# A pre-norm block with Hedgehog linear attention: where six query sums are inverted, and a new order for the first half

## The chip, the cores and the metric

The kernel runs on one core of a Trainium2 chip. The core has five engines with a queue of instructions each: TensorE (PE) multiplies matrices, VectorE (DVE), ScalarE (ACT) and GpSimd (POOL) do the rest of the arithmetic, and SyncE (SP) starts the transfers (DMAs). Each queue runs strictly in its own order; an instruction waits until the semaphores of what it needs have arrived, and everything behind it in the same queue waits with it. The metric is the device time of one execution in microseconds (us), lower being better.

## The reference

The input is 2048 tokens of width 640 in bfloat16. The block is an attention half and a feed-forward half, each with a residual:

```python
def _A_ref(x, wqkv, w_phi, wo):                  # 32 heads of 20
    q, k, v = split(x @ wqkv)
    pq = jnp.einsum("bhsd,hdf->bhsf", q, w_phi)
    pk = jnp.einsum("bhsd,hdf->bhsf", k, w_phi)
    phi_q = concat([softmax(pq), softmax(-pq)])  # 40 features a head
    phi_k = concat([softmax(pk), softmax(-pk)])
    kv = jnp.einsum("bhsf,bhsd->bhfd", phi_k, v)
    z  = jnp.einsum("bhsf->bhf", phi_k)
    num = jnp.einsum("bhqf,bhfd->bhqd", phi_q, kv)
    den = jnp.einsum("bhqf,bhf->bhq", phi_q, z)[..., None] + 1e-6
    return (num / den) @ wo
def _B_ref(x, w1, w2): return silu(x @ w1) @ w2  # 640 -> 1728 -> 640
h  = x + _A_ref(layernorm(x), ...)
h2 = h + _B_ref(layernorm(h), ...)
```

Because the output is a ratio, a common factor of the two halves of phi_q cancels. The kernel therefore leaves the positive exponentials of a query as they are and multiplies the negative ones by (sum of the positive ones) / (sum of the negative ones). That ratio is what the change is about: one number for each of 32 heads (33 columns with a padding head) and token.

## The kernel before, in words

The tokens are cut into 16 tiles of 128. The work of a tile is cut into named steps, and the whole program is one list of step names, `ORDER`. The list is walked once, each name issues its instructions to the queues, and the order in the list is the order within every queue. Nothing reorders it later. A table `ON` says for some steps on which engine they run. A number behind a name is the tile.

- Loading and norm. `X0, X1, X2, X4, X8` load the tokens (L161; `X8` brings tiles 8 to 15 in one transfer), `WKc` and `WVc` the weights (L164), `load0` to `load11` the rest (L488), all from SP's queue. `st` takes mean and variance on VectorE (L432, L433). `rs` is the inverse deviation: on GpSimd an addition and a power (L441, L444), on ScalarE a logarithm and an exponential (L438, L439). `xn` normalizes (L448), on VectorE or on GpSimd. `xt` transposes the tile: for tiles 0 to 3 on TensorE (L455) with a copy `x` behind it (L475), for the others by a DMA from SP's queue (L477).
- Folding weights. w_phi is multiplied into the key and the query weights before use. For keys: `wk` transposes on TensorE (L290), `wke` evicts (L307), `fk` multiplies (L314), `fke` evicts (L323). For queries: `wq0` to `wq5` transpose columns of wqkv by DMA (L386), `phq` builds the block diagonal of w_phi, `fq0` to `fq5` multiply (L398), `fqe` evict (L404).
- Keys and values. `K` and `V` project a tile (L496; for tile 0 in five pieces `K0.c` L523 and `V0.c` L508). `ex` takes both exponentials on ScalarE (L551), `su` their sums on VectorE (L555), `rk` inverts the sums on ScalarE by logarithm and exponential (L563, L564), `sc` scales on VectorE (L568), `ve` evicts the values (L572). `kv` adds the tile into the sum over all tokens (L587), which stays in two PSUM banks. After tile 15, `bd0` and `bd1` mask it into block diagonals (L596, L598).
- Queries. `Q` projects (L534), `qe` takes the exponentials (L656), `qs` the sums (L660), and `qr` is three VectorE instructions: a reciprocal (L668), a product that gives the ratio in bfloat16 (L670), and the scaling of the negative exponentials (L678). `qt` transposes the features by DMA (L684). `D` multiplies them into the masked sum (L709), `E` divides on VectorE (L721, L722), `ot` transposes (L733), `G` projects (L742) and `ga` adds the residual into `X` (L749).
- Feed forward. `ls`, `lr` and `hn` normalize again (L432, L441, L448), `ht` transposes by DMA (L769). Tiles go in units 0 to 1, 2 to 5, 6 to 9, 10 to 13, 14 to 15. `u0.*`, `u2.*` and so on are up projections (L824, L835), `s` the silu on ScalarE (L844, L851), `lt` a transpose (L856), `d` the down projections (L864, L867), `oa` the last addition (L873), `out` the store (L878).

PSUM has eight banks. Up to the step `halves`, two hold the key-value sum, and every `wk` pair, `xt`, `fk`, `fq`, `K`, `V` and `Q` takes the next of three pairs in turn, so it waits until what was put there three allocations earlier has been evicted. From `halves` on, eight single banks go round. Tiles in SBUF have small rings of buffers too: four for exponentials of keys, two for the sums of queries.

The up projections of unit 0 (the first `u0` in the list) need `ht0` and `ht1`. From `u2.2` on, after `G61 d11 ht5`, the two lists below are the same.

Of the kernel before, what the change touches and what calls it, by code (L numbers as in the profile page):

```python
# [18 lines left out]
warm0 warm1 warm2 warm3 warm4 warm5 warm6 warm7 warm8 warm9 warm10 warm11 warm12 warm13 warm14 X0 WK2  # L19
ones0 wk2 warm15 warm16 warm17 warm18 warm19 WK3 wke2 WK0 X1 WK1 st0 wk3 phi_a wke3 wk0 phi_b rs0 xn0  # L20
wke0 own st1 xt0 wk1 fk3 WK4 wke1 X2 wk4 rs1 WV0 wke4 x0 fk1 X4 fk3e WV3 xn1 st2 st3 rs2 WV2 WV4 rs3 fk0
fk1e fk0e fk4 WV1 V0.0 xn3 xn2 wph1 fk4e fk2 fk2e st6 xt1 wq2 K0s K0.0 K0.4 K0.3 K0.2 K0.1 ones1 x1 st4
rs4 xt2 K1 ex0 V0.2 ones5 xn4 wq4 V0.3 V0.1 st5 x2 wph0 su0 ex1 su1 rs5 V0.4 K2 xn5 phq xt3 V1 rs6 ex2
V2 x3 st7 xn6 rk0 X8 su2 rs7 ve1 ve2 ve0 xt4 sc0 st8 V3 fq2 xt5 rk2 ve3 K3 xn7 st11 ones3 fq2e V4 K4 rk1
ex3 wq3 ones2 ve4 kv0 ones6 sc1 ones7 sc2 V5 fq3 rs8 st9 ex4 su3 st10 rs9 wq0 kv1 ve5 ones4 xt6 su4 K5
fq0 fq3e K6 rk3 ex5 xt7 kv2 wq1 wq5 fq1 fq0e sc3 ex6 K7 load6 su5 fq1e mask kv3 ex7 xn8 st13 V6 xt8
mask0 rk4 ve6 rk5 su6 sc4 rs11 fq4 fq4e xn9 zeros st12 V7 ve7 rk6 V8 rs10 sc5 xt9 xn10 load3 V9 su7 ve8
fq5 rs12 rs13 st14 ve9 xt10 kv4 fq5e rk7 load7 K8 ex8 sc6 kv5 st15 xn11 K9 su8 xn12 sc7 Q0 kv6 K10 xt11
kv7 ex9 Q1 rk8 rs15 load2 su9 xn13 qe0 ex10 qe1 K11 xt13 sc8 rs14 mask1 rk9 qs0 kv8 xt12 xn14 load11 V10
V13 qr0 ex11 su10 sc9 xn15 V11 su11 kv9 xt14 rk10 ve13 ve10 K12 load4 ve11 qs1 K13 qr1 xt15 eqp K14 ex12  # L30
rk11 sc10 su12 kv10 ex13 ex14 rk12 V12 load5 V14 sc11 su13 ve12 K15 su14 pad0 sc12 rk13 kv11 qt0 Q2 sc13
ve14 qt1 load0 rk14 ex15 qe2 kv12 sc14 load1 su15 V15 kv13 rk15 ve15 Q3 qs2 kv14 load9 sc15 kv15 qr2 Q5
Q7 bd1 bd0 qe3 qe5 halves D0 qs3 Q4 qt2 E00 E01 qe7 qe4 qr3 D1 Q6 E10 Q9 E11 Q8 qe6 qe9 qs4 qr4 qs5 Q10
ot0 qr5 qt3 Q11 ot1 qe8 qe10 D2 qe11 E20 G00 G01 ga00 E21 D3 E30 qt4 E31 ga01 G10 ga10 ot2 G11 ga11 Q14
Q12 qe14 ot3 ls0 D4 lr0 G20 Q13 ls1 G30 qe12 lr1 hn0 qt5 E40 G21 G31 hn1 E41 ht0 ht1 ga30 ga20 qs6 Q15
qe13 pad1 ga21 D5 ga31 qs7 qr6 u0.0 E50 u0.6 qe15 E51 ls3 qr7 ls2 s0.0 load8 u0.L s0.L s0.6 u0.10 ot4
u0.12 u0.8 lr3 G40 G41 lr2 s0.12 s0.10 u0.4 load10 hn3 qt6 ga41 ot5 ga40 u0.2 s0.8 ls4 D6 lt0 G50 qt7
E60 lr4 G51 E61 ht3 ga51 s0.2 s0.4 d10 D7 ga50 hn4 ls5 ot6 lr5 hn2 qs8 d00 E70 hn5 oa00 ht2 d01 G60 ht4
G61 qr8 oa10 d11 ht5 ga61 u2.2 u2.0 ga60 qt8 E71 ot7 s2.0 oa01 qs9 u2.L qs13 s2.2 qr9 oa11 qs11 u2.6 D8
u2.10 E80 ls6 qt9 u2.7 u2.3 s2.L u2.11 s2.10 s2.6 qr13 E81 u2.9 s2.9 qr11 u2.5 qs12 s2.7 qs10 s2.3 u2.1  # L40
D9 G70 s2.5 E90 qr10 u2.12 s2.11 E91 ot8 G71 u2.4 lr6 ga71 ga70 qt11 out0 lt2 s2.1 qt10 u2.8 out1 hn6
s2.4 qr12 ls7 G80 s2.8 ga80 ot9 G81 D11 s2.12 E110 d30 ht6 qt13 E111 d20 D10 ga81 lr7 G90 E100 oa30 oa20
E101 ot10 G91 hn7 ga91 d31 ot11 ga90 ls8 qs15 lr8 d21 qt12 oa31 d50 G100 ls9 G101 hn8 out3 d40 d51 ht8
# [10 lines left out]
s14.8 out12 d140 d141 oa140 d150 oa141 out14 d151 oa150 out150 d152 oa151 out151 oa152 out152
# [4 lines left out]
def kernel(  # L59
# [603 lines left out]

    def query_ratio(t):
        n = HC * NCH
        s3 = sq.pop(t)[:].rearrange("p c (h b) -> p (c h) b", b=2)
# [1 line left out]
        nc.vector.reciprocal(rm[:], s3[:, :, 1])  # L668
# [1 line left out]
        nc.vector.tensor_tensor(  # L670
            r2[:],
            s3[:, :, 0].unsqueeze(2).to_broadcast([P, n, 2]),
            rm[:].unsqueeze(2).to_broadcast([P, n, 2]),
            op=ALU.mult,
        )
# [265 lines left out]
```

## Time and profile before

| | us |
|---|---|
| median of 3 runs | 237.36 |
| lowest and highest run | 237.30, 237.70 |
| the profiled execution | 236.82 |
| its span (first to last record) | 234.8 |
| busy in the span: PE, DVE, ACT, POOL | 229.5, 165.8, 105.1, 64.4 |

The profile is of one execution. A row of a timeline begins with the start and the duration in us; a row of the chain too. A row of a group ends with the count, then the busy time in all, the mean of one in ns, and the idle time in front. Durations of neighbours on one engine overlap slightly, so their sums come out a little too long. Matmuls are pipelined and their ends are modelled; what counts for PE is when it starts something and what it had to wait for.

### The profile page before, as it was taken

What the parts mean: (1) busy time and instruction counts of PE and PEld (TensorE: products, weight loads), DVE (VectorE), ACT (ScalarE), POOL (GpSimd) and SP (SyncE); (2) the same over time, 40 slices, a digit from 0 to 9 for tenths busy, and PEclk for the clock granted to TensorE, in tenths of its full rate; (3) what the DMA queues carried; (4) which work ended last, traced back from release to release, by engine and by line L of the source; (5) the groups of instructions that cost most, each with busy time, mean ns of one, the idle gap of its engine ahead of it and who ended that gap; (6) DMA issues with size and microseconds to landing.
All of it is one profiled execution on the core that took longest, in us unless ns stands there. A gap on an engine that the chain in (4) does not pass through costs nothing.

```text
span 234.8 us, 5031 instructions
## 1 busy us (share of the span) xinstructions
PE 229.5 (98%) x1984; PEld 161.2 (69%) x1984; DVE 165.8 (71%) x349; ACT 105.1 (45%) x222; POOL 64.4 (27%) x103
## 2 busy tenths in 40 slices
PE   8999989999999999999999999999999999999995
PEld 6777767777777777887545777645677455778874
DVE  3999979999999999999999795792472330404031
ACT  3999979877969754610234100054300326001410
POOL 5699999996000020121010111011020010100000
PEclk9999999999999999999999999999999999999999
DMA  6995379668976749694325946127313301011011
GB/s 165 346 228 138 88 162 149 181 59 172 245 270 73 155 94 159 148 120 95 81 64 133 163 97 173 31 56 176 72 24 88 98 0 28 30 29 56 8 56 56
DMA packets 67213, 26.79 MB, mean 114 GB/s; under 512 B 60151, under 2 KB 66167, under 8 KB 67063
## 3 DMA queue, kind: packets, MB, share of 16 engines
q1 hardware_dynamic: 66535, 26.47, 52.9%
q8 instruction: 15, 0.25, 0.5%
q10 hardware_dynamic: 656, 0.03, 0.2%
q14 instruction: 7, 0.06, 0.1%
HBM read 9.64 MB, written 2.62 MB: 52 GB/s over the span
## 4 chain that ended last, share of the span: by engine, by line
PE 87%; DVE 5%; DMA 3%; ACT 2%; issue 1%; POOL 1%; SPq 0%; DVEq 0%; POOLq 0%
PE banks L864 24%; PE banks L824 24%; PE banks L496 16%; PE banks L742 7%; PE banks L534 4%; PE banks L587 2%; PE banks L215 2%; PE banks L867 2%; PE banks L709 2%; DMA HnT<-xn 2%; DMA WTq<-in_A_wqkv_dram 1%; DVE Sq L660 1%; ACT Wfk L323 1%; PE banks L835 1%; DVE O L722 1%
## 5 line engine op out<-in xcount | busy, mean ns | idle before, releaser
L844 ACT ACTIVATE shT<-banks 128x512 bf16<-128x512 f32 (+1 forms) x53 | 28.7, 591 | 83.2 <-PE banks L824 83.2
L864 PE MATMUL banks<-w_sb,shT 128*128 128x320 bf16 (+2 forms) x429 | 61.3, 295 | 0.0
L824 PE MATMUL banks<-HnT,w_sb 128*128 128x512 bf16 (+1 forms) x325 | 59.0, 336 | 0.5 <-DMA HnT<-xn 0.5
L864 PEld LDWEIGHTS <-shT 128*128 128x128 bf16 x429 | 41.1, 98 | 15.2
L824 PEld LDWEIGHTS <-w_sb 128*128 128x128 bf16 x325 | 31.1, 98 | 22.8 <-issue 0.6
L441 POOL TENSOR_SCALAR rs<-mv 128x1 f32<-128x1 f32 x26 | 7.7, 298 | 137.1 <-DVE mv L433 136.9
L873 DVE TENSOR_TENSOR o_t<-banks,X 128x320 bf16<-128x320 f32 (+2 forms) x33 | 14.9, 474 | 39.6 <-PE banks L867 26.7
L496 PEld LDWEIGHTS <-XnT 128*128 128x128 bf16 x300 | 28.2, 98 | 10.5 <-DMA XnT<-xn 0.4
L448 POOL TENSOR_SCALAR xn<-X,mv,rs 128x640 bf16<-128x640 bf16 x12 | 31.0, 2586 | 0.4
L432 DVE BATCH_NORM_STATS2 st<-X 128x6 f32<-128x320 bf16 x64 | 27.9, 477 | 3.3 <-DMA X<-in_A_x_dram 3.2
L656 ACT ACTIVATE EQ<-banks 128x360 bf16<-128x360 f32 (+2 forms) x52 | 22.0, 514 | 8.4 <-PE banks L534 8.2
L742 PE MATMUL banks<-wo_sb,OT 128*128 128x320 bf16 x160 | 24.8, 299 | 0.0
L660 DVE TENSOR_REDUCE Sq<-EQ 128x66 f32<-128x1320 bf16 x16 | 24.1, 1517 | 0.0
L534 PE MATMUL banks<-Wfq,XnT 128*128 128x360 bf16 (+2 forms) x160 | 23.5, 299 | 0.0
L749 DVE TENSOR_TENSOR X<-banks,X 128x320 bf16<-128x320 f32 x32 | 14.5, 483 | 12.6 <-PE banks L742 12.5
L555 DVE TENSOR_REDUCE Sk<-EK 128x64 f32<-128x1280 bf16 x16 | 23.3, 1464 | 0.2
L551 ACT ACTIVATE EK<-banks 128x640 bf16<-128x640 f32 x32 | 20.8, 701 | 4.4 <-PE banks L496 2.0
L496 PE MATMUL banks<-Wfk,XnT 128*128 128x320 bf16 x150 | 22.5, 299 | 0.0
L496 PE MATMUL banks<-Wv,XnT 128*128 128x320 bf16 x150 | 21.8, 299 | 0.0
L742 PEld LDWEIGHTS <-OT 128*128 128x128 bf16 x160 | 15.1, 98 | 6.5
L534 PEld LDWEIGHTS <-XnT 128*128 128x128 bf16 x160 | 15.1, 97 | 6.2
L444 POOL TENSOR_TENSOR rs<-rs,nhalf_t 128x1 f32<-128x1 f32 x26 | 15.9, 613 | 2.2
(71 smaller groups left out, 203.9 us busy)
## 6 DMA issues: line engine op xcount, KB each, us to landing
out_dram<-o_t SPq DMA_DIRECT2D x15, 160.0 KB, 2.0
w_sb<-in_B_w_dram SPq DMA_DIRECT2D x5, 432.0 KB, 3.9
w_sb<-in_B_w_dram SPq DMA_DIRECT2D x3, 480.0 KB, 4.5
X<-in_A_x_dram SPq DMA_DIRECT2D x1, 1280.0 KB, 7.3
Wk<-in_A_wqkv_dram SPq DMA_DIRECT2D x5, 160.0 KB, 3.5
Wv<-in_A_wqkv_dram SPq DMA_DIRECT2D x5, 160.0 KB, 5.7
wo_sb<-in_A_wo_dram SPq DMA_DIRECT2D x1, 800.0 KB, 5.7
X<-in_A_x_dram SPq DMA_DIRECT2D x1, 640.0 KB, 5.9
```

Of the source, the lines that this page charges most:

```text
L432: nc.vector.bn_stats(st[:, i, :], X[:, t, i * HD : (i + 1) * HD])
L448: eng.tensor_scalar(out=xn_[t][:], in0=X[:, t, :], scalar1=mv_.pop(t)[:, 0:1], scalar2=rs_.pop(t)[:], op0=ALU.subtract, op1=ALU.mult,)
L496: nc.tensor.matmul(ps[:, g, 0:HD], XnT[:, c, t * P : (t + 1) * P], W[:, c, g * HD : (g + 1) * HD], start=(c == 0), stop=(c == C - 1),)
L534: nc.tensor.matmul(ps[:, 0 : e - a], XnT[:, c, t * P : (t + 1) * P], Wfq[:, c, a:e], start=(c == 0), stop=(c == C - 1),)
L551: nc.scalar.activation(E5[:, :, :, b, :], p4, AF.Exp, scale=sign)
L555: nc.vector.tensor_reduce(sk[t][:], ek[t][:, 0 : H * HF].rearrange("p (q f) -> p q f", f=DH), axis=AX.X, op=ALU.add)
L656: nc.scalar.activation(features(t, a, b)[:, :, :, i], p4, AF.Exp, scale=sign)
L660: nc.vector.tensor_reduce(sq[t][:], EQ[0][:, t, :, 0:FCH].rearrange("p c (q f) -> p c q f", f=DH), axis=AX.X, op=ALU.add)
L742: nc.tensor.matmul(ps[:, 0:HD], ot[t][:, c, :], wo_sb[:, c, g * HD : (g + 1) * HD], start=(c == 0), stop=(c == C - 1),)
L824: nc.tensor.matmul(ps[:, at : at + n], w1_sb[:, c, fc * P : fc * P + P], HnT[u][:, c, 0:n], start=(c == 0), stop=(c == C - 1),)
L844: nc.scalar.activation(shT[u][:, f0 * n : f1 * n], ps_of.pop(("u", u, f0))[:, 0 : (f1 - f0) * n], AF.Silu)
L864: nc.tensor.matmul(ps[:, 0 : b - a], shT[u][:, at : at + P], w2_sb[:, fc, a:b], start=(fc == 0), stop=False,)
```

## The change

The three instructions of `qr` become steps of their own for queries 0 to 5 (`EARLY_Q = 6`): `ql` inverts the sums of the negative exponentials on ScalarE with a logarithm and an exponential, `qi` multiplies on GpSimd, and only the scaling stays on VectorE as `qr`. For queries 6 to 15 `qr` still issues all three on VectorE.

In the table `ON`, the inverse deviations 1, 3, 4, 6, 7, 8, 9, 11, 12, 13 and 14 are now on ScalarE (before: 5, 6, 8, 9, 11 and 12); `xn5` goes from VectorE to GpSimd and `xn6` from GpSimd to VectorE; `wke2`, `x0` and `fq5e` go from ScalarE to VectorE.

The list `ORDER` is another one up to `u2.2`, in all queues. Cut to the places that matter:

```diff
 GpSimd's queue, first part:
-ones0 rs0 own rs1 rs2 rs3 xn3 ones1 rs4 ones5 xn4 phq xn6 rs7 xn7
+pad0 mask ones0 ones3 rs0 mask0 own ones5 rs2 ones1 xn3 xn4 rs5 xn5 phq ones2 ones7 xn7
 SP's queue, first part:
-X0 WK2 WK3 WK0 X1 WK1 WK4 X2 WV0 X4 WV3 WV2 WV4 WV1 wph1 wq2 wq4 wph0 X8 xt4 xt5 wq3 wq0 xt6 xt7 wq1 wq5 load6
+X0 WK2 WK3 WK0 X1 WK1 WK4 X2 WV0 X4 WV3 wph1 WV2 WV4 WV1 X8 wq2 wq3 wph0 xt4 wq1 load10 xt5 wq0 xt6 xt7 wq5 wq4
 PE's queue, keys and values:
-K1 V0.2 V0.3 V0.1 V0.4 K2 xt3 V1 V2 V3 fq2 K3 V4 K4 kv0 V5 fq3 kv1 K5 fq0 K6 kv2 fq1 K7 kv3 V6 fq4 V7 V8 V9
+K1 V0.3 V0.2 xt2 V1 V0.1 xt3 V0.4 K2 K3 V2 V3 kv0 K4 V4 fq3 kv1 V5 K5 fq0 K6 kv2 kv3 fq2 V6 fq1 K7 V7 V8 fq4 V9
 VectorE's queue, tiles 1 to 3 of the keys:
-su0 su1 xn5 st7 su2 sc0 st8 st11 sc1 sc2 st9 su3
+su0 st5 st9 st7 su1 sc0 st8 st12 xn6 sc1 su2 su3 sc2 sc3
 VectorE's queue, from the block diagonals to the second norm:
-qr2 bd1 bd0 qs3 E00 E01 qr3 E10 E11 qs4 qr4 qs5 qr5 E20 ga00 E21 E30 E31 ga01 ga10 ga11 ls0 ls1 hn0 E40 hn1
+bd1 bd0 qr2 qs3 E00 E01 E10 E11 qs5 qr3 qs4 E20 qr5 E21 ga01 ga00 ga10 qr4 ls0 E30 ga11 ls1 E31 hn0 hn1
 SP's queue, around it:
-ot3 qt5 ht0 ht1 load8
+ot3 ht1 ht0 load8
+    def query_inverse(t):
+        n = HC * NCH
+        rm = rq[t] = pools["att"].tile([P, n], F32, name="Rq")
+        if t < EARLY_Q:
+            nc.scalar.activation(rm[:], ratios(t)[:, :, 1], AF.Ln)
+            nc.scalar.activation(rm[:], rm[:], AF.Exp, scale=-1.0)
+        else:
+            nc.vector.reciprocal(rm[:], ratios(t)[:, :, 1])
+    def query_ratio(t):
+        rho[t] = pools["att"].tile([P, n, 2], BF16, name="Rho")
+        eng = nc.gpsimd if t < EARLY_Q else nc.vector
+        eng.tensor_tensor(rho[t][:], ..., op=ALU.mult)
+    def query_scale(t):
+        nc.vector.tensor_tensor(Em, Em, ..., op=ALU.mult)
-        add(f"qr{t}", lambda t=t: query_ratio(t))
+        if t < EARLY_Q:
+            add(f"ql{t}", lambda t=t: query_inverse(t))
+            add(f"qi{t}", lambda t=t: query_ratio(t))
+            add(f"qr{t}", lambda t=t: query_scale(t))
+        else:
+            add(f"qr{t}", lambda t=t: query_scaled(t))
```

The rows of the diff that begin with a queue's name show the steps of that queue in their order, taken out of the two lists.

More of the change, by code (lines that the diff above doesn't have):

```diff
@@ L18 @@
 ORDER = """
[L19 to L43, printed above, removed]
@@ L54 @@
[L54 removed]
+warm0 warm1 warm2 warm3 warm4 warm5 warm6 warm7 warm8 warm9 warm10 warm11 warm12 warm13 warm14 pad0 mask
+ones0 ones3 X0 st0 WK2 WK3 phi_a WK0 wk2 warm15 warm16 warm17 warm18 warm19 rs0 X1 phi_b WK1 WK4 wk3
+wke2 wke3 wk0 wke0 xn0 xt0 X2 mask0 st1 wk1 wke1 fk3 wk4 x0 WV0 fk1 rs1 X4 fk3e fk1e fk2 xn1 own fk0 WV3
+fk2e wke4 st2 V0.0 ones5 fk0e fk4 wph1 st3 xt1 K0s fk4e WV2 rs2 K0.2 x1 WV4 K0.1 st4 K0.0 xn2 K0.4 rs3
@@ new lines @@
+K0.3 ones1 ex0 K1 st6 V0.3 WV1 V0.2 rs4 su0 X8 xt2 V1 V0.1 ex1 xn3 xn4 x2 ve1 xt3 x3 wq2 V0.4 ve0 st5
+rs5 K2 rk0 st9 st7 K3 wq3 su1 ex2 ex3 sc0 V2 ve2 wph0 rk1 st8 xn5 phq V3 xt4 rs9 st12 ve3 rs6 wq1 rs7
+load10 kv0 ones2 xn6 K4 ex4 V4 sc1 fq3 ones7 ve4 rs8 kv1 xn7 xt5 wq0 xn8 xn9 fq3e xt6 V5 su2 xt7 wq5 rk2
+su3 ve5 rk3 wq4 K5 sc2 ex5 fq0 K6 kv2 sc3 st11 kv3 fq0e xt8 fq2 ex6 st10 su4 fq2e su5 rs11 V6 ve6 st13
+fq1 K7 st14 V7 fq1e rk4 xt9 rs10 xn10 ex7 zeros ve7 su6 rs13 V8 sc4 ve8 fq4 V9 ones4 load0 xt10 load5
@@ new lines @@
+ve15 sc15 qs2 kv15 bd1 load9 qe3 Q5 Q7 halves ql2 qe5 qe7 bd0 qi2 qr2 qs3 D0 E00 E01 D1 E10 ql3 Q4 E11
+qe4 qt2 Q9 qi3 Q6 qe9 qs5 ql5 D2 qi5 Q8 ot0 ot1 qr3 G00 G01 qs4 qe6 E20 qr5 E21 ql4 G10 ga01 Q10 qe8 qi4
+ga00 qe10 ga10 qt3 Q11 D3 qr4 qt5 ls0 G11 qe11 Q14 Q12 E30 Q13 lr0 ot2 qe14 ga11 qe12 qe13 ls1 qt4 E31
+hn0 lr1 ot3 Q15 G20 hn1 ht1 qs6 G21 qe15 qs7 ht0 D5 G30 load8 pad1 ga20 qr6 ga21 ga30 G31 load11 E50 E51
+D4 u0.12 E40 u0.4 u0.0 s0.0 s0.12 ga31 ls3 u0.6 E41 ot5 qs8 u0.L u0.2 ls2 qr7 s0.6 u0.8 qt6 lr2 s0.4 ot4
```

74 lines of the change are left out of this document (46 added, 28 removed).

## Prediction

> **What bounds the kernel now.** I read the page first, then what PE waited for, then the chain of waits.
>
> ```profile
> span 234.8 us, 5031 instructions
> PE banks L398 <- DMA WTq<-in_A_wqkv_dram: 1.0, 1, 1.0
> PE banks L824 <- DMA HnT<-xn: 0.5, 1, 0.5
> ```
>
> ```profile
> 7.96 2.52 ACT Wfk L323 x4
> 10.52 1.52 PE banks L523 x10
> ...
> 28.51 2.91 DMA WTq<-in_A_wqkv_dram
> 31.47 0.44 PE banks L398 x5
> ...
> 88.86 3.74 DMA HnT<-xn
> 92.73 2.34 PE banks L824 x20
> ```
>
> PE is the bound nearly everywhere. From 10.52, the first matmul of `K0`, to the end it streams and stops twice: 1.0 us for a transposed query weight (`wq1`, needed by `fq1` at 31.47) and 0.5 us for the transpose of the second norm (`ht1`, needed by `u0.0` at 92.73). Ahead of 10.52 the chain runs through ScalarE's evictions of the folded key weight. The change moves matmuls but neither adds nor removes one, so the new time is the old one plus what happens to four things: the start, these two stops, new stops, and the tail, whose order stays. Behind the start there is no more than 1.5 us to gain. How full the other engines are, by two stretches:
>
> ```profile
> 30.00:60.00 30.00, 28.91 (x299) 21.54 (x298) 27.73 (x37) 25.15 (x55) 26.08 (x21) 1.00 0.82 154
> 72.00:95.00 23.00, 22.48 (x215) 16.96 (x213) 22.18 (x52) 15.13 (x42) 2.18 (x5) 1.00 0.72 124
> ```
>
> The columns behind the length are the busy time of PE, its weight loads, VectorE, ScalarE and GpSimd, then the granted clock (1.00). ScalarE has 4.9 us free in the first and 7.9 in the second; VectorE has 2.3 and 0.8, and GpSimd is full in the first and nearly empty in the second.
>
> **The change part by part.** First the stop at `fq1`: SP's queue, transfers to landing, GpSimd, and two of PE's projections (`V5` and `K6`).
>
> ```profile
> 23.48 4.98 SPq L477 DMA_TRANSPOSE XnT<-xn  x2
> 28.51 2.58 SPq L386 DMA_TRANSPOSE WTq<-in_A_wqkv_dram  x2
> XnT<-xn SPq DMA_TRANSPOSE x12, 3.1
> L448 POOL TENSOR_SCALAR xn<-X,mv,rs 128x640 bf16<-128x640 bf16 x12 | 31.0, 2586 | 0.4
> L444 POOL TENSOR_TENSOR rs<-rs,nhalf_t 128x1 f32<-128x1 f32 x26 | 15.9, 613 | 2.2
> 4.43 0.53 POOL L441 TENSOR_SCALAR rs<-mv 128x1 f32<-128x1 f32 x1 [1.69 <-DVE mv L433]
> 24.99 1.52 PE L496 MATMUL banks<-Wv,XnT 128*128 128x320 bf16 x10
> ...
> 28.57 1.52 PE L496 MATMUL banks<-Wfk,XnT 128*128 128x320 bf16 x10
> ```
>
> `wq1` reads only DRAM, but it stood in SP's queue behind `xt6` and `xt7`, which waited for norms on GpSimd (2.59 us each). It went out at 28.51 and landed 2.91 later. Now it stands directly behind `xt4`. GpSimd does `xn3` from 12.0, as before, to 14.6 and `xn4` to 17.2, so `wq1` goes out near 18.5 (1.3 for a transpose, 2.58/2) and lands near 21.4, and `fq1` itself comes a little later than before. The stop goes: −1.0.
>
> What is late next is a transposed tile of tokens, since `wq1` and `load10` now precede `xt5`, and `xn5` takes 2.59 on GpSimd instead of 0.5 on VectorE. Up to `V5` the two orders have the same steps but one `kv` more (about 0.3): `V5` at 25.3; up to `K6` the same less one `fq`: 28.3. GpSimd goes on with `rs5` (at most 0.53 + 0.61) to 18.3 and `xn5` to 20.9, and `xt5` lands 3.1 later, at 24.0: 1.3 early. `xt6` then needs `xn6`, now on VectorE, whose deviation comes from ScalarE behind `ve3` at about 23; it goes out at 23.4 and lands at 26.5: 1.8 early. The later ones have more room, since GpSimd loses five inverse deviations, 5 × 0.9 us. New stops here: 0, with bounds 0 and 1.0 (the deviation and the norm half a microsecond slower each and the transposes one).
>
> Next VectorE and the stop at `u0`: what leaves VectorE, and the like on ScalarE.
>
> ```profile
> L668 DVE RECIPROCAL Rq<-Sq x16: 310/356/366, 48.5 to 155.4; 128x33 f32<-128x33 f32 x16
> L670 DVE TENSOR_TENSOR Rho<-Sq,Rq x16: 228/228/488, 48.9 to 155.7; 128x66 bf16<-128x66 f32 x16
> L563 ACT ACTIVATE Sk<-Sk x16: 257/258/280, 17.9 to 65.6; 128x64 f32<-128x64 f32 x16
> L564 ACT ACTIVATE Rk<-Sk x16: 309/310/312, 18.2 to 65.9; 128x128 bf16<-128x128 f32 x16
> L438 ACT ACTIVATE rs<-mv,eps_t x6: 279/296/326, 15.0 to 39.0; 128x1 f32<-128x1 f32 x6
> L439 ACT ACTIVATE rs<-rs x6: 203/203/204, 15.4 to 39.4; 128x1 f32<-128x1 f32 x6
> ```
>
> The middle of the three numbers is the median in ns. VectorE loses 6 × (0.356 + 0.228) = 3.5 us. `x0`, `wke2` and `fq5e` come to it; `xn6` for `xn5` is even. ScalarE gets 6 × (0.258 + 0.310) = 3.4 at most, since it inverts 33 numbers and not 64, and 5 × 0.50 = 2.5 for the five more deviations, and gives up three copies: some 4 us over stretches with 4.9 and 7.9 free, beside other work. A GpSimd product of 66 elements has no row. Between VectorE's 0.23 and the 0.61 of GpSimd's power I take the middle, 0.4. From the end of a `qs` to its `qr` the new way needs 0.26 + 0.31 + 0.4, about 1.0; in VectorE's new order at least another query's sum, its scaling and part of an `E` stand between the two, over 2 us. So it costs nothing there; were that cover gone, 1.0 in place of 0.6 on VectorE's chain each time.
>
> From `bd0` to `hn1` VectorE worked without a break:
>
> ```profile
> 69.93 0.24 DVE L598 SCALAR_TENSOR_TENSOR KVB<-banks,mask 128x18 bf16<-128x18 f32 x1
> ...
> 87.51 0.26 DVE L721 RECIPROCAL Rd<-banks 128x18 f32<-128x18 f32 x1
> 87.80 0.53 DVE L722 TENSOR_TENSOR O<-banks,Rd 128x360 bf16<-128x360 f32 x1
> 88.25 0.52 DVE L448 TENSOR_SCALAR xn<-X,mv,rs 128x640 bf16<-128x640 bf16 x1
> ```
>
> The new list takes from this stretch the reciprocals and ratios of `qr3`, `qr4` and `qr5` (3 × 0.58 = 1.8) and the half of `E4` ahead of `hn1` (88.25 − 87.51 = 0.7), and puts the scaling of `qr2` in (0.5): 2.0 shorter. It also begins earlier. `qr2`, 1.1 with all three instructions, no longer stands ahead of `bd0`, and PE brings `kv15` 1.0 earlier; between 1.1 and 2.1 I take 1.6. `hn1` then ends at 88.8 − 3.6 = 85.2. `ht1` goes out there, `ht0` 1.3 behind it, and with the 3.74 above it lands at 90.2, or 90.6 with `ot3` just ahead of both. PE, 1.0 early, comes to `u0` at 92.73 − 0.52 − 1.0 = 91.2. So the second stop goes too: −0.5, with 0.6 to spare; bounds −0.5 and 0 (a transpose a microsecond longer). Between `u0` and `u2.2` both orders have the same steps, so VectorE's and PE's arrivals move together; for single banks emptied late on the way I keep 0 to 0.3.
>
> The start:
>
> ```profile
> L235 POOL MEMSET w_last<- 64x640 bf16 x2 | 1.3, 626 | 0.1
> ...
> L245 POOL MEMSET mask<- 128x378 f32 x1 | 0.7, 690 | 0.0
> ```
>
> GpSimd now fills `pad0`, `mask` and `ones3` before `rs0`: 0.63 + 0.69 and two small ones, in a wait of 1.69. `wke2` goes into VectorE's own wait for `rs0`. Ahead of the `fke`, ScalarE drops one copy (`x0`, about the 0.63 of an `fke`, 2.52/4) and takes `rs1` (0.50). `K0` still needs the fourth `fke`. So it starts at 10.5: 0, with bounds −0.2 and +0.3 (GpSimd late).
>
> **Sum.** −1.0 − 0.5 + 0 at the start + 0 for new stops (at most 1.3) = −1.5. The profiled execution took 236.82, its span and 2.0 around it; that gives 235.3. The median of the runs shown, 237.36, is 0.54 higher, and the same step from there gives 235.8. A measurement of this kernel tells about 0.2%, 0.5 us, from no change.
>
> **The rivals.** *Only the first stop goes.* If GpSimd's products held VectorE up by as much as the change takes from it, 6 × 0.6, the second norm would come as late as PE does, and 0.5 stays: 236.3. Against it: VectorE's `sc`, two SBUF inputs, took 0.80 in the middle of two GpSimd norms of 2.5 each, which leaves no room for a wait for either's end.
>
> ```profile
> 40.75 0.80 DVE L568 TENSOR_TENSOR EK<-EK,Rk 128x1280 bf16<-128x1280 bf16 x1
> 39.06 5.00 POOL L448 TENSOR_SCALAR xn<-X,mv,rs 128x640 bf16<-128x640 bf16 x2
> ```
>
> The Trainium skill, SBUF — State Buffer, section "Who interferes with whom", says that a VectorE instruction with two SBUF inputs contends with a GpSimd instruction that reads SBUF, and that the first holds the shared port for its whole instruction. By that rule this `sc` would have waited up to 2.5 us and the result would be this rival's; the trace does not agree for this pair.
>
> *The wait moves.* `fq1` no longer waits, but `V5` or `K6` does: `xt5` behind `rs5` and `xn5`, and `xt6` stuck behind it in SP's queue. They would have to be over 2 us later than worked out, and 1.0 to 1.5 comes back: 236.8 to 237.3. For it: GpSimd has no break there.
>
> *Slower: `X8`.* `st9` needs tile 9 and now stands third behind `su0` in VectorE's queue, at about 16, ahead of `su1` and `sc0`.
>
> ```profile
> 11.79 0.65 SPq L161 DMA_DIRECT2D X<-in_A_x_dram  x1
> X<-in_A_x_dram SPq DMA_DIRECT2D x1, 1280.0 KB, 7.3
> ```
>
> It landed at 19.1. Two transposes and a small load no longer go out ahead of it (2.58 + 0.65), so it goes out near 8.5 and, with the same 7.3, lands at 15.8; it also has less in front of it. If it still landed at 19.1, VectorE would stand for 3.1 us, and `sc0`, `sc1` and `xn6` behind it would make PE wait for all but the 1 us that they have to spare, with a second wait for `xt6` of about 1: 235.8 + 3.1 = 238.9. It decides the sign when `X8` lands past some 18.5, that is 1.5 + 1 later than worked out.
>
> The Trainium skill, DMA: Bandwidth & Descriptors, section "Queues, rings and completion order", says that on each DMA engine a queue's descriptors are consumed in ring order. By that rule `X8` comes directly behind the `WV` loads, and the result is the 235.8.
>
> **How the numbers follow.** Both stops gone, 235.8, own range 235.2 to 236.2: 0.52. One gone, or half a microsecond lost at a tight place, 236.3, up to 236.8: 0.19. The wait moves, 236.8 to 237.7: 0.13. Slower by `X8` or another late transfer, up to 239: 0.16. Faster by over 0.2% (below 236.9) are the first two and a little of the third, 0.72; the same 0.11; slower 0.17. The range 235.2 to 237.7 leaves out the last case and what lies below the first.
>
> **What would show it.** Right: PE has no wait for `WTq`; `K0` starts at 10.3 to 10.8; `u0` starts at 91.0 to 91.4 without a wait for `HnT`; VectorE waits for `X` only at the first tile; GpSimd's products take 0.23 to 0.6 and the pair on ScalarE 0.5 to 0.6. A new row in which PE waits for `XnT`, `EK` or `EqT`, or a span above 234.3, would make me wrong.

## The result and the profile after

The changed kernel takes 234.73 us (median, 234.53 to 234.74), the kernel before in the same comparison 237.33 (237.12 to 237.70). The ratio is 0.9887, with a 95% interval from 0.987 to 0.9904. That is 2.6 us, 1.1%. The prediction said 1.5 less, with 235.2 as its lower end: the sign was right, the size too small. Medians and ratios here and below leave out three executions, two of e5 and one of e14, that had a lower granted clock (0.993) and took 238.2 us or more.

First the span and what PE waited for in the kernel after, the rows that answer the first fence of the prediction (the last three numbers of a row are the wait in all, how often, the longest):

```profile
span 232.8 us, 5040 instructions
PE banks L217 <- PEq L951: 0.8, 1, 0.8
PE banks L292 <- DMA Wk<-in_A_wqkv_dram: 0.6, 2, 0.4
PE banks L457 <- DVE xn L450: 0.2, 1, 0.2
PE banks L525 <- ACT Wfk L325: 0.2, 1, 0.2
```

Every wait that is left lies at the start, up to `K0` (L525). No row for `WTq` or `HnT` is left, and none for `XnT`, `EK` or `EqT` has come. Lines of the changed kernel have higher numbers than those of the kernel before, by 2 up to the queries' sums and by 15 to 26 behind them. The two stretches that the prediction showed, PE, weight loads, VectorE, ScalarE and GpSimd in turn:

```profile
30.00:60.00 30.00, 30.00 (x319) 22.73 (x318) 29.32 (x39) 27.49 (x65) 23.39 (x18) 1.00 0.82 184
72.00:95.00 23.00, 23.00 (x220) 17.63 (x219) 21.83 (x49) 16.61 (x47) 3.06 (x7) 1.00 0.66 128
```

PE is full in both (28.91 and 22.48 before). In the first, VectorE rose from 27.73 to 29.32 although instructions were taken from it: without stops the list advances faster, and more of it lies in the same 30 us (319 matmuls against 299). Next PE's timeline at the places of the two old stops, before and then after:

```profile
29.93 0.50 PE L587 MATMUL banks<-VP,EK 128*128 128x63 bf16 x11
31.47 0.44 PE L398 MATMUL banks<-phi_q,WTq 128*128 128x120 bf16 x5 [1.04 <-DMA WTq<-in_A_wqkv_dram]
...
91.72 0.50 PE L709 MATMUL banks<-KVB,EqT 128*128 128x63 bf16 x11
92.73 1.47 PE L824 MATMUL banks<-HnT,w_sb 128*128 128x256 bf16 x12 [0.52 <-DMA HnT<-xn]
```

```profile
10.78 1.52 PE L525 MATMUL banks<-Wfk,XnT 128*128 128x320 bf16 x10 [0.16 <-ACT Wfk L325]
...
32.23 0.43 PE L400 MATMUL banks<-phi_q,WTq 128*128 128x120 bf16 x5
...
90.40 0.50 PE L734 MATMUL banks<-KVB,EqT 128*128 128x63 bf16 x11
90.74 2.45 PE L850 MATMUL banks<-HnT,w_sb 128*128 128x256 bf16 x21
```

The bracket of a row is the idle time ahead of it, counted from the modelled end of the matmuls before. The starts say more. In the kernel after, a group of eleven such matmuls (x11) occupies PE for 90.74 − 90.40 = 0.34 us until the next one starts. Before, 31.47 − 29.93 − 0.34 = 1.20 us were lost at `fq1`, not 1.0, and 92.73 − 91.72 − 0.34 = 0.67 at `u0`, not 0.5.

Counted so, the span can be split into the start of `K0` and what follows. Before, 234.8 − 10.52 = 224.3 us follow; after, 232.8 − 10.78 = 222.0. In every profile of the changed kernel in which PE did not stop behind `K0` the second part is 222.0 or 222.1 us, wherever `K0` started. It serves as a ruler below: what a kernel needs beyond 222.0 behind `K0` is what PE lost there.

### The profile page after: what moved, and what is told of

It reads as the page before. It is cut to its first block, busy times and chain, and to the rows that moved or that the text cites. A ratio compares the mean times of both kernels' runs of the same rounds, so it can differ in the third digit from the quotient of the medians.

```text
span 232.8 us, 5040 instructions
## 1 busy us (share of the span) xinstructions
PE 228.0 (98%) x1977; PEld 160.5 (69%) x1984; DVE 164.0 (70%) x340; ACT 107.4 (46%) x241; POOL 62.6 (27%) x99
## 4 chain that ended last, share of the span: by engine, by line
PE 95%; DMA 2%; SPq 1%; issue 1%; ACT 1%; DVE 0%
PE banks L890 24%; PE banks L850 24%; PE banks L498 18%; PE banks L536 9%; PE banks L767 9%; PE banks L589 2%; PE banks L734 2%; PE banks L893 2%; DMA Wk<-in_A_wqkv_dram 2%; PE banks L861 1%; PE banks L525 1%; PE banks L400 1%; ACT Wfk L325 1%; SPq L166 1%; PE banks L510 0%
## 5 line engine op out<-in xcount | busy, mean ns | idle before, releaser
L850 PE MATMUL banks<-HnT,w_sb 128*128 128x512 bf16 (+1 forms) x318 | 58.4, 335 | 0.4
L443 POOL TENSOR_SCALAR rs<-mv 128x1 f32<-128x1 f32 x21 | 5.8, 276 | 113.2 <-DVE mv L435 113.2
L498 PE MATMUL banks<-Wv,XnT 128*128 128x320 bf16 x150 | 22.5, 299 | 0.0
L747 DVE TENSOR_TENSOR O<-banks,Rd 128x360 bf16<-128x360 f32 (+1 forms) x32 | 15.7, 491 | 1.1
```

The costliest lines, as they stand in the source:

```text
L498: nc.tensor.matmul(ps[:, g, 0:HD], XnT[:, c, t * P : (t + 1) * P], W[:, c, g * HD : (g + 1) * HD], start=(c == 0), stop=(c == C - 1),)
L850: nc.tensor.matmul(ps[:, at : at + n], w1_sb[:, c, fc * P : fc * P + P], HnT[u][:, c, 0:n], start=(c == 0), stop=(c == C - 1),)
```

## The experiments

Each row is one kernel; the ratio is to the kernel before on the same chip, with its interval.

| kernel | ratio | median us | `K0` starts | span − `K0` |
|---|---|---|---|---|
| before, as predicted from | 1 | 237.3 | 10.52 | 224.3 |
| b0: before again | 0.999 [0.9965, 1.0016] | 237.39 | 10.55 | 224.5 |
| e1: before, `wq1` early | 1.0028 [1.0009, 1.0047] | 237.66 | 11.78 | 223.2 |
| e2: before, queries 2 to 5 divided | 0.9991 [0.9963, 1.0019] | 237.11 | 11.10 | 225.7 |
| e3: both | 1.0014 [0.9994, 1.0035] | 237.30 | 11.06 | 224.1 |
| e10: e3 and six `rs` on ScalarE | 1.0114 [1.0061, 1.0167] | 239.86 | 13.29 | 223.1 |
| e11: e3 and four `rs` on ScalarE | 1.0004 [0.9979, 1.003] | 237.81 | 10.67 | 224.5 |
| after | 0.9887 [0.987, 0.9904] | 234.73 | 10.78 | 222.0 |
| a0: after again | 0.9882 [0.9842, 0.9921] | 234.95 | 11.09 | 222.0 |
| a1: after again | 0.9882 [0.9849, 0.9915] | 235.20 | 10.70 | 223.0 |
| a2: after again | 0.9903 [0.9886, 0.9919] | 234.65 | 10.85 | 222.1 |
| e4: after, nothing divided | 1.001 [0.9993, 1.0026] | 237.42 | 10.63 | 225.6 |
| e5: after, `wq1` late | 0.9887 [0.9841, 0.9933] | 235.20 | 10.60 | 223.1 |
| e6: after, `rs` as before | 0.992 [0.9892, 0.9949] | 235.41 | 10.47 | 223.3 |
| e7: after, `fk0e` on VectorE | 0.9894 [0.985, 0.9939] | 235.03 | 11.42 | 222.0 |
| e8: after, queries 3 to 5 not divided | 0.9945 [0.9916, 0.9974] | 235.80 | 10.83 | 223.0 |
| e9: after, `X8` later | 0.9958 [0.9936, 0.998] | 236.34 | 10.54 | 223.7 |
| e12: after, `phq` later | 0.9899 [0.9882, 0.9916] | 234.57 | 10.56 | 222.0 |
| e13: after, `X8` in halves | 0.9898 [0.988, 0.9916] | 234.50 | 10.56 | 221.9 |
| e14: both | 0.9894 [0.9878, 0.9911] | 234.46 | 10.90 | 222.0 |

The last two columns are of one profiled execution each. The start varies from one profile to the next by more than these edits explain: 10.52 to 11.78 in kernels whose first 10 us are those of before, 10.54 to 11.09 in those with the start of after, and the edit of e1 lies 8 us behind it.

### Parts of the change put into the old order

**e1**, the query weight early:

```diff
-... xt4 sc0 st8 ... xt7 kv2 wq1 wq5 ...
+... xt4 wq1 sc0 st8 ... xt7 kv2 wq5 ...
```

> The kernel before with one step moved: wq1 from behind xt7 to directly behind xt4. Read from start to start in the trace of before, the stop at fq1 is 1.20 us (kv2 started at 29.93 and takes 0.34, fq1 started at 31.47), not the 1.04 of the list of waits. Theory A: from fq1 on VectorE hangs on the same stop (fq1's eviction, the exponentials of tile 7 and rk4 stand behind it on ScalarE, and VectorE waited 1.7 for rk4 at 35.45), so both move and the kernel gains 1.2 us, 0.9 to 1.4, with the stop at u0 left at 0.67. Theory B: VectorE is full from there to the second norm whatever PE does, so u0 starts at 92.7 as before and the gain is lost in a longer stop there: 0 to 0.3 us. A third: xt5, one transpose later in the queue, holds V5: no gain.

**e2**, four queries divided over ScalarE and GpSimd, in the order of before:

```diff
-... qs2 kv14 load9 sc15 kv15 qr2 ... qs3 Q4 ... qs4 qr4 qs5 Q10 ot0 qr5 ... E20 ...
+... qs2 ql2 qi2 kv14 load9 sc15 kv15 qr2 ... qs3 ql3 qi3 Q4 ... qs4 ql4 qi4 qs5 ql5 qi5 qr4 Q10 ot0 ... E20 qr5 ...
+    EARLY_Q = (2, 3, 4, 5)
```

> The kernel before with the inversion on ScalarE and the product on GpSimd for queries 2 to 5 alone (GpSimd is still busy with norms when queries 0 and 1 come), ql and qi directly behind their qs, qr4 behind qs5 and qr5 behind the first half of E2 so that neither stands right behind its own sum. fq1 keeps its stop. If VectorE's instructions are what delays u0, 4 x 0.58 = 2.3 us less bring ht0 down well before PE's arrival, the stop of 0.67 (start to start) goes, perhaps the 0.15 at kv14 too: 0.7 to 0.8 us faster. If GpSimd's product or ScalarE's inversion costs VectorE as much as it saves, nothing: 0 to 0.2 us.

**e3**, both edits:

> Both edits of the two runs before. If the two stops add up, 1.20 + 0.67 and up to 0.15 at kv14: 1.9 to 2.0 us faster, most of what the whole change gives, with before's order otherwise. If the rest of the new order matters by itself, clearly less: 1.0 to 1.5.

**b0**, the kernel before once more, for the spread:

> The kernel before, unchanged, profiled a second time beside the changed one. In the three partial edits K0 started at 11.1 to 11.8 instead of 10.5, two of them behind a wait for the first piece of Wv, although nothing was changed in any queue ahead of 18 us. Theory A: the landing of the first loads varies from execution to execution (Wv's first piece 4.3 to 6.3 us after its issue), in every kernel; then this second profile can show a K0 anywhere from 10.5 to 11.8 and stops at fq1 and u0 that shrink by as much as K0 is late. Theory B: it belongs to the edited kernels; K0 at 10.5 and the two stops of 1.20 and 0.67 again.

In b0 PE waited 1.3 us for `WTq` and 0.3 for `HnT`: the two stops vary in size. None of e1, e2 and e3 is faster. What PE waited for, without the start rows, in e1, e2 and e3:

```profile
PE banks L824 <- DMA HnT<-xn: 0.4, 1, 0.4
PE banks L587 <- DVE EK L568: 0.3, 1, 0.3
```

```profile
PE banks L400 <- DMA WTq<-in_A_wqkv_dram: 1.9, 1, 1.9
PE banks L850 <- DMA HnT<-xn: 1.2, 1, 1.2
```

```profile
PE banks L498 <- DMA XnT<-xn: 1.3, 1, 1.3
```

In e1 the stop for `WTq` is gone and behind `K0` PE is 1.1 us better than before. In this profile `K0` started 1.26 us later than before, behind a wait for `Wv`, which takes that back; why the median of its twelve runs is no better either, the one profile does not settle. In e3 both old stops are gone, and a new one of 1.3 us stands at `V13`. There GpSimd is the limit, at work without a break on deviations and norms, and the transpose of tile 13 goes out only when its norm is done:

```profile
44.52 0.57 POOL L446 TENSOR_TENSOR rs<-rs,nhalf_t 128x1 f32<-128x1 f32 x1
45.08 2.51 POOL L450 TENSOR_SCALAR xn<-X,mv,rs 128x640 bf16<-128x640 bf16 x1
...
47.61 3.30 SPq L479 DMA_TRANSPOSE XnT<-xn  x2
```

e2 and e3 also correct what the prediction held for the cause of the stop at `u0`. The profile of e2 is of its slowest execution (238.77, median 237.11), so the rows are those of e3. VectorE is not full ahead of `hn1` any more; in both it stood 1.94 us for PE, and 0.28 and 0.47 for GpSimd's products:

```profile
81.22 0.27 DVE L746 RECIPROCAL Rd<-banks 128x18 f32<-128x18 f32 x1 [1.94 <-PE banks L734]
...
89.29 0.72 DVE L450 TENSOR_SCALAR xn<-X,mv,rs 128x640 bf16<-128x640 bf16 x1
```

Yet `hn1` ends at 90.0, later than before (88.8). From the end of the block diagonals to the end of `hn1` VectorE needs 19.3 us here, 18.6 before and 16.8 after. What it stood for is `D2`. In PE's old list `D2` stands behind five projections in a row (`Q6 Q9 Q8 Q10 Q11`), in the new one behind three (`Q4 Q9 Q6`): it starts at 80.77 in e3, at 79.80 before and at 74.38 after. So in the old order relief for VectorE alone does not bring `u0` its input earlier. No run moves `D2` by itself.

**e10**, e3 with six inverse deviations on ScalarE as well: three parts of the change in the old order. Queries 0 and 1, `rs5`, `xn5`, `xn6` and the three copies stay as before.

```diff
-rs1="POOL" rs3="POOL" rs4="POOL" rs7="POOL" rs13="POOL" rs14="POOL"
+rs1="ACT"  rs3="ACT"  rs4="ACT"  rs7="ACT"  rs13="ACT"  rs14="ACT"
```

> The kernel before with three parts of the change but its own order otherwise: wq1 directly behind xt4, queries 2 to 5 divided over ScalarE and GpSimd, and rs1, rs3, rs4, rs7, rs13, rs14 on ScalarE. If the loads and placements alone carry the gain: no stop for XnT, HnT or WTq, ratio 0.988 to 0.992. If the new order of the steps is needed as well (each part removed so far only moved the wait): a wait turns up somewhere else, at the start, for EK or for XnT, ratio 0.996 to 1.004.

This was slower, and by a mistake of placing: in the old order `rs3` stands ahead of the folded key weights in ScalarE's queue, and its input came from VectorE only at 10.94:

```profile
10.94 0.29 ACT L440 ACTIVATE rs<-mv,eps_t 128x1 f32<-128x1 f32 x1 [1.74 <-DVE mv L435]
...
11.38 1.86 ACT L325 CAST Wfk<-banks 128x640 bf16<-128x640 f32 x3
```

**e11**, the same with `rs1` and `rs3` left on GpSimd:

> The kernel before in its own order with three parts of the change: wq1 directly behind xt4, queries 2 to 5 divided over ScalarE and GpSimd, and rs4, rs7, rs13, rs14 on ScalarE; rs1 and rs3 stay on GpSimd, so that nothing stands ahead of the folded key weight on ScalarE. If these parts carry the gain: K0 near 10.5 to 11.1, no stop above 0.4 us behind it, ratio 0.987 to 0.992. If the new order is needed as well: a stop of 0.5 us or more for EK, XnT or HnT, ratio 0.995 to 1.002.

```profile
PE banks L498 <- ACT XnT L477: 1.0, 1, 1.0
...
PE banks L498 <- ACT VP L574: 0.3, 1, 0.3
PE banks L589 <- DVE EK L570: 0.3, 1, 0.3
```

`K0` starts at 10.67, and all the old stops are gone, the one for `XnT` of e3 too. In their place ScalarE stands 1.77 us for tile 4's mean ahead of `rs4`, its copy of a transposed tile comes late, and PE stops for it; two smaller stops follow. 224.5 us behind `K0`, the same as before. So these parts gain nothing in the old order: here an instruction put on an engine with free time held that engine's queue, because it stood there before its input had come.

### Parts taken out of the new order

**e4**, all six queries' inversion and product on VectorE again:

```diff
-    EARLY_Q = 6
+    EARLY_Q = 0
-... ql0 ... qi0 ... ql5 ... qi5 ...
```

> The changed kernel with EARLY_Q = 0: all sixteen ratios on VectorE again, in the new order, all else as changed. VectorE gets 2 x 0.58 ahead of the block diagonals, where the changed kernel has 0.4 us to spare, and 4 x 0.58 before hn1, less the 0.5 that it waits there: hn1 1.5 to 2.9 later than 85.3. ht0 landed at about 89.8 to 90.8 and PE came at 90.74, so u0 stops for 0.8 to 2 us: 235.5 to 236.7. If the order alone gives the gain, it stays at 234.7.

**e8**, the same for queries 3, 4 and 5 only (`EARLY_Q = 3`):

> The changed kernel with queries 3, 4 and 5 inverted and multiplied on VectorE again, at their qr steps; queries 0 to 2 stay divided over ScalarE and GpSimd. Theory (VectorE's unbroken stretch from bd0 to hn1 sets u0): VectorE gets 3 x 0.58 = 1.8 us back ahead of hn1; with 0.6 us to spare PE waits some 0.5 to 1.2 us at Q, G or u0: ratio 0.990 to 0.994. Rival (the queries 0 to 2 are the costly ones, because they stand among the steps that feed kv): no new stop, 0.986 to 0.989.

What PE waited for in e4, and then its timeline in e8:

```profile
PE banks L536 <- DVE O L747: 0.9, 1, 0.9
PE banks L767 <- DMA OT<-O: 0.9, 1, 0.9
...
PE banks L589 <- DVE EK L570: 0.7, 1, 0.7
```

```profile
88.81 0.50 PE L734 MATMUL banks<-KVB,EqT 128*128 128x63 bf16 x11
89.97 1.26 PE L767 MATMUL banks<-wo_sb,OT 128*128 128x320 bf16 x8 [0.66 <-DMA OT<-O]
```

The new order without the division is no faster than before; even its fastest execution, 236.78, is 2 us above the changed kernel. Not all of the 3.6 us that this profile lost behind `K0` is the division's: the wait for `EK`, some 0.9 from start to start, comes from a late `X8` (it landed at 17.97) and is explained with the slower rival below. With queries 0 to 2 divided the new order has about half of its gain, with one stop of 89.97 − 88.81 − 0.34 = 0.82 us ahead of `u0`. Here VectorE is the limit, as the prediction had it. Division and order need one another, as far as the runs go: in the old order only queries 2 to 5 were divided.

**e6**, the inverse deviations back where they were (`rs1`, `rs3`, `rs4`, `rs7`, `rs13`, `rs14` on GpSimd, `rs5` on ScalarE):

> The changed kernel with six inverse deviations (rs1, rs3, rs4, rs7, rs13, rs14) back on GpSimd and rs5 back on ScalarE. Theory (GpSimd's chain of norms was the next limit behind the query weight, as the run with both stops removed showed at V13): GpSimd gets some 5 x 0.9 = 4.5 us more between 12 and 52, its norms end up to 4 us later, xn13 and xn15 above all, and PE waits once or more for XnT: ratio 0.992 to 1.002. Rival (GpSimd still has room, the placement was free): no stop for XnT and 0.986 to 0.990, as the changed kernel.

```profile
PE banks L457 <- POOL xn L450: 0.6, 1, 0.6
PE banks L498 <- DMA XnT<-xn: 0.2, 1, 0.2
```

It loses 1.3 us behind `K0`, in the range expected, but not at the end of GpSimd's chain: PE stops early, once for `xn3` itself (at 16.37) and once, by 0.2, for a transposed tile. The interval of its ratio overlaps those of the changed kernel, so the loss is shown by the profile and not by the times.

**e5**, `wq1` back behind `xt7`:

```diff
-... rs6 wq1 rs7 ... xt7 wq5 ...
+... rs6 rs7 ... xt7 wq1 wq5 ...
```

> The changed kernel with one step moved back: wq1 from behind xt4 to behind xt7, as in the kernel before. wq1 then goes out near 28.3 and lands near 31.3; fq1, which the new PE order puts behind kv3, fq2 and V6, starts at 32.2. If the new place of fq1 among the matmuls was enough, the time stays within 0.2 us of the changed kernel (a transpose fewer ahead of xt5 could even help). If wq1's place in SP's queue is what removed the stop, 0.5 to 1.2 us slower than the changed kernel.

```profile
28.48 3.89 SPq L388 DMA_TRANSPOSE WTq<-in_A_wqkv_dram  x3
```

Where `wq1` stood is not what removed the stop at `fq1`. Here it goes out at 28.48, as late as before (28.51), and with a landing some 2.9 us later it is there at 31.4. PE does not wait for it, because in the new order `fq1` comes later: at 33.1 here and 32.2 in the kernel after, 31.5 before with its stop. The 1.1 us that this profile lost behind `K0` are a wait for `EK`, which is the subject of the next part. The ratios of e5 and a0, on the same chip, are 0.9887 and 0.9882, so no cost of the late `wq1` is shown.

**e7**, one eviction of a folded key weight from ScalarE to VectorE (`fk0e="DVE"`), to bring `K0` forward:

> The changed kernel with one eviction of the folded key weight, fk0e, on VectorE instead of ScalarE. K0 waits for the fourth of five evictions on ScalarE (8.09 to 10.6); with three ahead and one beside them on VectorE at about 9.3, K0 should start 0.4 to 0.6 us earlier, and if nothing behind it is late the whole is that much faster: 234.2. VectorE gets 0.75 us before the second tile's statistics; if xn2 or the sums then come late, 0, or up to 0.5 us slower.

No gain: VectorE brought the piece later, `K0` started at 11.42, and 222.0 us followed as ever.

**a0**, the changed kernel again beside these:

> The changed kernel, unchanged, a second time: 0.987 to 0.990 of before again, with a span within 0.4 of 232.8 if its order is less exposed to late loads, executions within 0.5 us of each other; if late loads hit it as they hit the partial edits, up to 1.2 us more in some executions and K0 after 11.

### The slower rival: `X8` and the wait for `EK`

**e9**, the load of tiles 8 to 15 one transposed weight later in SP's queue:

```diff
-... su0 X8 xt2 ... x3 wq2 V0.4 ...
+... su0 xt2 ... x3 wq2 X8 V0.4 ...
```

> The changed kernel with the load of tokens 8 to 15 (X8) one transposed weight later in SP's queue. It goes out about 2.0 us later and lands near 19, and VectorE waits for it some 2.9 us instead of 0.9, with su1, sc0 and xn6 behind it. The prediction's slower rival: PE then loses what is above 1 us of it, 1 to 2 us: ratio 0.992 to 0.997. Rival (there is more room than worked out, since VectorE makes it up before PE needs xt6 and kv0): 0.986 to 0.990.

**a1**, the changed kernel a third time:

> The changed kernel once more, for the comparison on this chip: ratio 0.986 to 0.990, PE without a stop above 0.4 us behind K0.

In the profile of a1, unlike those of after and a0, PE stopped for `EK` at `kv0`. Its chain of waits up to there (start, duration, what):

```profile
8.43 9.43 DMA X<-in_A_x_dram
...
17.88 0.90 DVE st L434 x2
...
21.35 1.36 DVE EK L570
```

The mechanism is the prediction's slower rival: `X8` lands, `st9` waits for it, and `su1`, `sc0` and `kv0` follow. But the `EK` step, `sc0`, took 1.43 us where it takes 0.82 otherwise. **a2** is the changed kernel a fourth time, on the same chip as the three edits that follow:

> The changed kernel on the same chip: ratio 0.986 to 0.990. Where X8 lands later than about 17.4 and phq starts before sc0, sc0 takes 1.2 to 1.8 us and PE waits 0.6 to 0.9 for EK at kv0; where sc0 starts first there is no wait.

GpSimd's product `phq` and VectorE's `sc0` in the timelines of after, a1, a2 and e5, and `sc0` in that of e9, in this order:

```profile
21.01 1.33 POOL L369 TENSOR_TENSOR phi_q<-WPQ,own_q 120x600 bf16<-120x600 bf16 x1
20.48 0.82 DVE L570 TENSOR_TENSOR EK<-EK,Rk 128x1280 bf16<-128x1280 bf16 x1
```

```profile
20.84 1.19 POOL L369 TENSOR_TENSOR phi_q<-WPQ,own_q 120x600 bf16<-120x600 bf16 x1
21.27 1.43 DVE L570 TENSOR_TENSOR EK<-EK,Rk 128x1280 bf16<-128x1280 bf16 x1
```

```profile
17.71 0.89 DVE L434 BATCH_NORM_STATS2 st<-X 128x6 f32<-128x320 bf16 x2 [1.37 <-DMA X<-in_A_x_dram]
21.25 1.71 POOL L369 TENSOR_TENSOR phi_q<-WPQ,own_q 120x600 bf16<-120x600 bf16 x1
21.10 0.82 DVE L570 TENSOR_TENSOR EK<-EK,Rk 128x1280 bf16<-128x1280 bf16 x1
```

```profile
17.55 0.89 DVE L434 BATCH_NORM_STATS2 st<-X 128x6 f32<-128x320 bf16 x2 [1.50 <-DMA X<-in_A_x_dram]
20.88 1.19 POOL L369 TENSOR_TENSOR phi_q<-WPQ,own_q 120x600 bf16<-120x600 bf16 x1
20.94 1.81 DVE L570 TENSOR_TENSOR EK<-EK,Rk 128x1280 bf16<-128x1280 bf16 x1
```

```profile
22.15 0.81 DVE L570 TENSOR_TENSOR EK<-EK,Rk 128x1280 bf16<-128x1280 bf16 x1
```

Of the two, the one that starts second is held. `phq` alone takes 1.19 (e9) and `sc0` 0.82. In a1 and e5 `phq` is first and `sc0` ends 0.67 and 0.68 behind it, less than its own length: it was let go some 0.15 us ahead of the end of `phq`. In a2 `sc0` starts 0.15 ahead and keeps its 0.82, and `phq` takes 1.71, ending 1.04 behind `sc0`; the same 1.04 in the profile of after. The profile of e4 has the collision too: `sc0` started 0.59 behind `phq`, took 1.27 and ended 0.67 behind it. So the landing at 17.7 in a2 did no harm and the one at 17.55 in e5 did. In e9 they do not meet, since `phq` ran from 20.68 for 1.19; `X8` is late by itself there, VectorE waits 2.07 us for it up to 18.76, and PE stops 1.2 us at `kv0` with `sc0` at its usual length.

**e12** moves `phq` behind two small fills in GpSimd's queue, **e13** loads tiles 8 to 11 at the old place and 12 to 15 behind `wq3`, **e14** does both:

```diff
-... xn5 phq V3 ... kv0 ones2 xn6 ... fq3 ones7 ve4 ...
+... xn5 ones2 ones7 phq V3 ... kv0 xn6 ... fq3 ve4 ...
```

```diff
-    add("X8", lambda: load_x(8, 16))
+    add("X8", lambda: load_x(8, 12))
+    add("X12", lambda: load_x(12, 16))
```

> The changed kernel with the small fills ones2 and ones7 ahead of phq in GpSimd's queue instead of behind it, so that GpSimd's product of two SBUF inputs starts some 0.4 us later, at 21.3 to 21.5. If this product holds sc0, sc0 starts first in most executions and takes 0.8 us, not 1.4 to 1.8, and the wait for EK at kv0 falls to 0.3 us or less, also where X8 lands at 17.5 or later; fewer executions above 235, ratio 0.985 to 0.989. If the landing alone makes the wait, it stays at 0.7 to 0.9 in such an execution.

> The changed kernel with the load of tokens 8 to 15 in two halves: tiles 8 to 11 at the old place, tiles 12 to 15 behind wq3. 640 KB took 5.9 us from issue to landing where 1280 KB took 8.4, so tile 9 is there near 14.7 to 15.5 and VectorE does not wait for it; sc0 starts near 19.6 to 20.0, ahead of phq, and takes 0.8 us. No wait for EK at kv0; ratio 0.985 to 0.988 and no execution above 235.2. If the second half comes too late for st12, VectorE waits there and the gain is lost: 0.988 to 0.992.

> Both edits, X8 in halves and phq behind the small fills. If both causes act and each edit is enough, the same as with the halves alone: 0.985 to 0.988, no wait for EK.

None of the three profiles has a wait for `EK`. In e12 `X8` landed at 17.4, `sc0` started at 20.79, 0.1 ahead of `phq`, and kept 0.81, while `phq` took 1.75. The fills put `phq` back by some 0.2 us and not by the 0.4 expected: it started at 20.89, where `xn5` ended at 20.74. That was enough in this one profile. In e13 VectorE had no wait for `X` behind 12.03. The medians, 234.46 to 234.57, are below that of a2 on the same chip, 234.65, by less than the runs can tell apart, so neither edit is shown to beat the changed kernel; the profile of a2 has no collision either. Nor does the ruler leave much: 222.0 us behind `K0` is PE without a stop.

## Why the prediction was right in sign and too small

- **The first term, −1.0 at `fq1`.** The stop went and cost 1.20. `wq1` went out at 18.86 (predicted 18.5). The reason given, `wq1` directly behind `xt4`, is enough in the old order (e1), but in the new one the stop is gone without it (e5), because `fq1` comes later. That this term came out was in part luck.
- **The second term, −0.5 at `u0`.** The stop went and cost 0.67. `hn1` ended at 84.11 + 1.20 = 85.3 (predicted 85.2) and PE came to `u0` at 90.74 (91.2). The reason was half of it: VectorE's unbroken work limits the new order (e4, e8), but in the old order with VectorE relieved `hn1` still ended at 90.0 (e3), because `E2` waited for `D2`. The new list brings `D2` forward by 5.4 us, which the prediction did not look at.
- **"0 for new stops", no term for small ones.** Two further losses of before went too. `V7` to `V9`, thirty matmuls, should take three times 1.36 (30.87 to 32.23 in the kernel after) and took 0.21 more until the next group, and the pair of `kv` at 67.35 took 0.15 more than 0.68. The list of waits has no row for either. In b0 they are 0.27 and 0.16. What PE waited for there stays open.

The rows of before, in its timeline:

```profile
35.06 4.46 PE L496 MATMUL banks<-Wv,XnT 128*128 128x320 bf16 x30
39.35 0.28 PE L398 MATMUL banks<-phi_q,WTq 128*128 128x40 bf16 x5
...
67.35 0.99 PE L587 MATMUL banks<-VP,EK 128*128 128x63 bf16 x22
68.18 1.99 PE L534 MATMUL banks<-Wfq,XnT 128*128 128x360 bf16 x13
```

- **The start, 0.** It was +0.26 (10.78), inside the bounds given, and inside what the start varies by anyway.
- **The sum.** −1.20 − 0.67 − 0.21 − 0.15 + 0.26 = −1.97, the change of the span, 2.0. The failed step is "−1.0 − 0.5 = −1.5" together with "behind the start there is no more than 1.5 us to gain": both took PE's losses from the list of waits, which showed 1.5 of 2.23 us. The last step of the sum, the offset, is short by about as much.
- **The offset.** "The same step from there" took the one profiled execution of before, 236.82 with a span of 234.8, as typical of where time is lost. It was a quick one. The 104 executions of before that were run beside the other kernels have a median span of 235.3, and the 21 of the changed kernel 232.7, where its profiled one has 232.8. So a usual execution of before loses 0.5 us more than the profiled one, and the change saves that too: 2.6 and not 2.0. Where this half microsecond goes is not shown. A longer stop at `fq1` fits: from start to start it was 1.20 us in the profile of before, 1.46 in b0 and 2.0 in e2, where `wq1` stands at its old place.
- **The transposed tiles, bounds 0 and 1.0.** Right: `xn5` ended at 18.53 + 2.52 = 21.05 (predicted 20.9) and PE stopped for no `XnT`. With the deviations back on GpSimd PE stops for `xn3` and once for `XnT` (e6).
- **ScalarE and GpSimd.** The pair on ScalarE took 0.24 and 0.23 in the median, less than the 0.57 taken as the most. GpSimd's product, taken as 0.4 with bounds 0.23 and 0.61, has a median of 0.36 and a largest of 0.95, where VectorE's `sc` ran at the same time (53.93 to 54.74); in a0 that one took 1.36. Neither held PE up.

```profile
L682 POOL TENSOR_TENSOR Rho<-Sq,Rq x6: 312/362/952, 52.4 to 77.1; 128x66 bf16<-128x66 f32 x6
```

- **"VectorE waits for X only at the first tile": wrong.** `X8` went out at 8.67, near the 8.5 predicted, but took 8.4 us and not 7.3. VectorE waited 0.89 for it, and PE lost nothing by it.

```profile
17.09 0.89 DVE L434 BATCH_NORM_STATS2 st<-X 128x6 f32<-128x320 bf16 x2 [0.89 <-DMA X<-in_A_x_dram]
```

- **The slower rival.** It is real, and was priced too high. With `X8` at 18.76 (e9) the time is 236.3 and the gain is not gone; 238.9 for a landing at 19.1 is not borne out. A landing at 17.7 cost nothing in a2; at 17.55 and 17.88 PE waited 0.9 and 0.75 us, mostly because `sc0` met `phq`.
- **The rule on the shared port.** The prediction set aside the rule of the Trainium skill, SBUF — State Buffer, section "Who interferes with whom", on one row: `sc` took 0.80 in the middle of GpSimd's norms. That `sc` started at 40.75, 1.69 us behind the start of its norm. Other rows of the same trace do show the rule at work:

```profile
35.04 2.52 POOL L448 TENSOR_SCALAR xn<-X,mv,rs 128x640 bf16<-128x640 bf16 x1
35.45 1.14 DVE L568 TENSOR_TENSOR EK<-EK,Rk 128x1280 bf16<-128x1280 bf16 x1 [1.67 <-ACT Rk L564]
```

Here `sc` started 0.41 behind the norm and took 1.14; at 28.93 it started 0.57 behind one and took 0.98. Both ended 1.55 us behind the start of the norm, which is 0.73 + 0.82: the norm held it for its first 0.73 us. In all profiles the sum of the two is 1.54 or 1.55 for an `sc` that started 0.22 to 0.58 behind a norm of this length, and an `sc` that started 0.83 or more behind one took 0.77 to 0.83. And in the trace of before a norm that started 0.11 behind an `sc` (19.77) took 3.10 in place of 2.52. So the traces agree with the section that the two instructions contend and that one of them waits. They do not agree with its "for the whole instruction", which stands there with VectorE's two-port modes and which the prediction took for this pair: a norm of 2.5 us held `sc` for 0.73, `phq` of 1.19 us for 1.04. Nor was it always the first that won: in a2 a norm that started 0.15 ahead of an `sc` (40.18) was the one held, to 3.17. The prediction's mistake was to take one row, late in a norm, for all. It did not change the forecast, but it hid what the collision with `phq` later showed.

## What to carry to other kernels

Measure what PE lost from start to start of its groups, over the whole span, and not from the list of waits: here 2.2 us stood behind a list of 1.5. Ask too whether the profiled execution is a usual one: this one was half a microsecond quicker than the median. When several chains of nearly equal length feed a bound engine, removing one stop alone moves the wait to the next chain (e1 to e3, e11), and here only moving the work and its order together removed them all; the division was worth nothing alone (e2), and without it most of the gain was gone (e4). Before moving an instruction to an engine with free time, ask when its input arrives, since it blocks everything behind it there (e10: `K0` 2.6 us later than in e11), and what it meets on the other engine while it runs.
